# Ring swaps on VectorE, idle-time products on TensorE, table loads behind gates, and the merged tail tiles moved, in an FFT-and-MLP kernel

## The chip, the core and the metric

The program runs on one core of one Trainium2 chip. The core has TensorE (PE in the profile, its weight loads PEld), VectorE (DVE), ScalarE (ACT), GpSimd (POOL) and the queue engine SyncE (SP), and 16 DMA engines that serve transfers issued from SP and from POOL. The metric is the device time of one execution in microseconds (us). Before the change the median of 13 runs is 872.5 us (871.04 to 877.49).

## What is computed

Inputs are x (8 batches of 3008 x 256), complex 256 x 256 weights with biases, and the two matrices of a hidden layer of 2048. Per batch: a real FFT over the 3008 positions, a complex linear layer, a soft threshold, an inverse FFT; then a two-layer network with a squared ReLU on all 24064 rows.

```
X  = rfft(x, axis=1)
Yr = Xr @ w_r - Xi @ w_i + b_r
Yi = Xr @ w_i + Xi @ w_r + b_i
Y  = sign(.) * max(|.| - 0.01, 0)          # on Yr and Yi
y  = irfft(Y).reshape(24064, 256)
out = (s * relu(y @ w_in)**2 + b) @ w_out
```

## The kernel before

The FFT of 3008 = 94 x 32 positions is done as matrix products. A table `A_t` (first DFT over 94), block tables `F_t` and `F_2` (forward over 32, with twiddles), `T_t` (inverse over 32) and `C_t` (inverse over 94) are constants in DRAM. `F_c` and `T_c` are their compact forms as loaded; `place_f` copies `F_c` into `F_t` on ScalarE and into `F_2` on VectorE, `place_t` copies `T_c` into `T_t` on VectorE.

**The first batch** goes through `first_batch`, with nothing beside it. x comes in four chunks (`emit_load_x`, GpSimd's queue); for each chunk 16 products (L320) make `ut`, which ScalarE and VectorE move out of PSUM (L158, L162). SyncE loads everything else at the same time: the weights `w_st`, the biases, `F_c`, `T_c`, the identity and so on, with no wait between them. After the last chunk stand `place_f`, `place_t`, and then 12 steps, each with `mix` (L357), `fwd_dft` (L388), a soft threshold (`m` on ScalarE, L393, and `z` on VectorE, L395), `inv_dft` (L406), and later turns and last DFTs (L421, L438). In `mix` the result `g` leaves PSUM on VectorE (L367) in two steps of three, and on ScalarE (L364) in the third. GpSimd makes `W_g`, `low` and `high` from the weights and biases in between, and loads x of the second batch and `w_in`, `w_out` behind a one-element copy that waits for `T_c`.

**The steady part** is a list of 48 row tiles of the network. A tile has 16 slots; in a slot stand two products of the first layer (L689), the ReLU (L696 on ScalarE), its square (L703 on VectorE or L700 on ScalarE, whichever a running count `load` finds less busy), and four products of the second layer for the tile before (L758). The FFT of later batches is cut into small units that `schedule` spreads over these slots: `s1_units` (first DFT), `s23_units` (forward DFT, complex mix, threshold, inverse DFT, in 12 rounds), `s4_units` (last DFT). In `s23_units`, `mix_unit(i)` ends with four VectorE operations on a buffer `ring` (L563, L568, L569, L570), whose result `t` is brought into another layout `z` by four DMAs of 32 KB each on SyncE's queue (L576): rows 64j.. of half r go to rows 64r.. of half j. `inv_unit(i)` multiplies `z` (L585); its result goes to DRAM (`vd`) and comes back as `vs`. The last rounds of a batch, 10 and 11, have no other unit between them and their `inv_unit` but a few of the same kind.

**The order of tiles** comes from `_tile_order`: three wide tiles per half of the first two batches, then five tiles of 512 rows per batch; what remains of two batches together makes two tail tiles of 512 and 384 rows, which follow in the next free place. The last two tails stand at the very end. A tail tile stores its result in many small DMAs (L742), a main tile in two of 128 KB per pair of sub-tiles (L722). Each engine runs its instructions in program order; SyncE issues its DMAs in order too.

Of the kernel before, what the change touches and what calls it, by code (L numbers as in the profile page):

```python
# [9 lines left out]
F16 = mybir.dt.float16  # L10
# [4 lines left out]
P = 128  # L15
# [57 lines left out]
def _tile_order(nb):  # L73

    tiles = []
    rest = []
    for b in range(nb):
        if b < 2:  # L80
            for h in range(2):
                tiles += [("wide", b, (h, lo), w) for lo, w in ((0, 32), (32, 32), (64, 30))]
            continue
        tiles += [("main", b, j, 512) for j in range(5)]
        pr, half = divmod(b, 2)
        if half == 1:
# [8 lines left out]
def kernel(  # L95
# [82 lines left out]
    def emit_load_x(b):  # L178
        xv = x[b].rearrange("(n1 n2) d -> n1 (n2 d)", n2=N2)
        for c in range(N2 // XCH):  # L180
# [3 lines left out]
            )  # L184
            x16[(b, c)] = t


    A_t = cpool.tile([P, 96], F16, name="A_t")
    nc.sync.dma_start(out=A_t[0:N1, :], in_=A_d)
# [14 lines left out]
    nc.sync.dma_start(out=F_c.rearrange("p q r k -> p q (r k)"), in_=F_d)  # L204
    b_h = cpool.tile([P, D], F16, name="b_h")
    nc.vector.memset(b_h, 0.0)

# [4 lines left out]
    nc.sync.dma_start(out=T_c, in_=T_d)  # L212

    nc.sync.dma_start(out=sel_t, in_=S_d)
    eye_t = cpool.tile([P, P], F16, name="eye_t")
    nc.sync.dma_start(out=eye_t, in_=E_d)
    C_t = cpool.tile([96, 96], F16, name="C_t")
    nc.sync.dma_start(out=C_t, in_=C_d)

    b_st = rpool.tile([P, 2, D], F32, name="b_st", tag="rt")  # L220
    for i, bv in enumerate((b_r, b_i)):
        nc.sync.dma_start(out=b_st[:, i], in_=bv.unsqueeze(0).to_broadcast([P, D]))
# [5 lines left out]
    nc.sync.dma_start(out=s_bc, in_=moe_s.unsqueeze(0).to_broadcast([P, 1]))  # L228
    nc.sync.dma_start(out=bb_bc, in_=moe_b.unsqueeze(0).to_broadcast([P, 1]))
# [12 lines left out]

    neg_lam = cpool.tile([P, 1], F32, name="neg_lam")
    nc.vector.memset(neg_lam, -LAM)
    ones = cpool.tile([P, P], F16, name="ones")
    nc.vector.memset(ones, 1.0)
# [21 lines left out]
    def blocks(t):  # L268
        return t.rearrange("p q (r a k) -> p q r a k", r=2, a=2)
# [5 lines left out]
    def place_f():  # L275
        for a in range(2):
            r = slice(64 * a, 64 * a + 64)
            nc.scalar.copy(out=blocks(F_t)[r, :, :, a], in_=F_c[r])

            for h, f in enumerate(F_2):  # L280
                q = slice(h * H, h * H + H)
                nc.vector.tensor_scalar_mul(
                    out=blocks(f)[r, :, 0, a], in0=F_c[r, q, 1], scalar1=-1.0
                )
                nc.vector.tensor_copy(out=blocks(f)[r, :, 1, a], in_=F_c[r, q, 0])

    def place_t():
        for i in range(4):
            r = slice(32 * i, 32 * i + 32)
            c = 64 * (i % 2)  # L290
            nc.vector.tensor_copy(out=T_t[r, :, c : c + 64], in_=T_c[r])  # L291

    def make_bias():
        ps = other_bank()
# [17 lines left out]
    def first_batch():  # L312
        ut = ypool.tile([P, DC, 96, N2], F16, name="ut", tag="yt")
        last_dve = last_act = None
        for c in range(N2 // XCH):
            for dc in range(DC):
                ps = two_banks()
                for j in range(XCH):
                    lo = j * D + dc * P
                    nc.tensor.matmul(  # L320
                        ps[:, j // 4, (j % 4) * 96 : (j % 4) * 96 + 96],
                        x16[(0, c)][0:N1, lo : lo + P], A_t[0:N1, :],
                        start=True, stop=True,
                    )
# [187 lines left out]
    def s23_units(b):  # L512
# [40 lines left out]
        def mix_unit(i):  # L553
            ps = one_bank().rearrange("p (r e) -> p r e", r=2)
            xt = xf.pop(i)
            for r in range(2):
                for dc in range(DC):
                    nc.tensor.matmul(  # L558
                        ps[:, r, :], xt[:, 2 - r, dc], W_g[:, dc, r],
                        start=(dc == 0), stop=(dc == DC - 1),  # L560
                    )
            t, m = ring[0][:, i % 4], ring[0][:, 4 + i % 2]
            nc.vector.tensor_tensor(  # L563
                out=t, in0=ps, in1=hold[i // 2][:, i % 2].unsqueeze(1).to_broadcast([P, 2, D]),
                op=ALU.add,
            )
# [3 lines left out]
            nc.vector.tensor_tensor(out=t, in0=t, in1=m, op=ALU.subtract)  # L570
            load["dve"] += 1.75

            z = ring[0][:, 6 + i % 6]
            for j in range(2):
                for r in range(2):
                    nc.sync.dma_start(  # L576
                        out=z[64 * r : 64 * r + 64, j], in_=t[64 * j : 64 * j + 64, r]
                    )
            zt[i] = z

        def inv_unit(i):
# [266 lines left out]
```

## Time and profile before

| | value |
|---|---|
| median of 13 runs | 872.5 us |
| the profiled execution: its own time | 871.9 us |
| the profiled execution: its span | 870.0 us |
| PEld / ACT busy | 599.0 / 641.4 us |
| VectorE busy | 694.1 us, 971 instructions |
| SyncE ring DMAs (L576) | 336 |
| HBM traffic | 52.54 MB read, 46.66 MB written |

Busy time is a union per engine; times in a timeline count from the start of the span. In a row of a timeline the first number is the start, the second how long the merged piece lasted, and a bracket at the end tells how long the engine stood idle before it and what ended that. A row of windows gives busy time per engine (with the number of instructions), then the mean granted TensorE clock (1.00 is full), the mean share of the 16 DMA engines and their rate in GB/s. The record of the clock begins 20.6 us into the span; before that the rows read 1.00 whatever it was, and the pace of the products tells.

### The profile page before, as it was taken

To read this page: it belongs to the slowest core of one execution; us is meant where nothing else is said; L and a number is where in the kernel's file an instruction comes from. 1 tells how busy PE (TensorE), PEld (TensorE's weight loads), DVE (VectorE), ACT (ScalarE), POOL (GpSimd) and SP (SyncE) were. 2 spreads that over 40 slices of the span, in tenths; PEclk is the share of its full clock that TensorE was granted. 3 is DMA by queue.
4 is the path that set the end of the run, shared out by engine and by line. 5 is a ranking of instruction groups with operands and counts; after the bars stand their busy time and mean duration, and the time that the engine had idled before them with its cause. 6 is when DMAs were issued, how large, how long until landed. Compare 5 with 4: busy or idle time off the path is not lost.

```text
span 870.0 us, 16955 instructions
## 1 busy us (share of the span) xinstructions
PE 837.9 (96%) x6580; PEld 599.0 (69%) x6580; DVE 694.1 (80%) x971; ACT 641.4 (74%) x848; POOL 32.7 (4%) x53
## 2 busy tenths in 40 slices
PE   4889989999999999999999999999999999999996
PEld 3756766777667766777667776777667777766665
DVE  6788977888778887888878988798877888776664
ACT  4687877687677886787777787787877777666662
POOL 5110000000000000000000000000000000000000
PEclk9999999999999999999999999999999999999999
DMA  8754366423664248522764236623374133411111
GB/s 189 128 121 119 90 157 159 140 57 78 168 151 129 80 113 217 136 64 74 176 169 117 70 97 158 180 86 86 83 193 118 50 86 105 114 31 38 37 39 53
DMA packets 109347, 96.90 MB, mean 111 GB/s; under 512 B 10319, under 2 KB 101715, under 8 KB 107923
## 3 DMA queue, kind: packets, MB, share of 16 engines
q1 hardware_dynamic: 103266, 81.41, 32.7%
q0 software_dynamic: 6000, 14.42, 10.2%
q8 instruction: 51, 0.84, 0.4%
q14 instruction: 30, 0.24, 0.1%
HBM read 52.54 MB, written 46.66 MB: 114 GB/s over the span
## 4 chain that ended last, share of the span: by engine, by line
PE 89%; DMA 4%; ACT 3%; DVE 2%; issue 1%; SPq 0%; POOL 0%; DVEq 0%; POOLq 0%
PE psh L689 36%; PE psa L758 36%; PE psf L558 4%; PE psf L493 3%; DMA ring<-ring 3%; PE psf L529 2%; PE psf L544 2%; PE psf L585 2%; PE psf L638 2%; DMA x<-in_x_dram 1%; ACT rt L696 1%; DVE T_t L291 1%; ACT yt L158 0%; PE psh L357 0%; ACT m L393 0%
## 5 line engine op out<-in xcount | busy, mean ns | idle before, releaser
L696 ACT ACTIVATE rt<-psh 128x1024 f32<-128x1024 f32 (+2 forms) x384 | 387.3, 1009 | 120.7 <-PE psh L689 119.0
L703 DVE TENSOR_TENSOR gt<-rt 128x1024 f16<-128x1024 f32 (+2 forms) x322 | 386.2, 1201 | 110.6 <-ACT rt L696 110.1
L758 PE MATMUL psa<-w_out_t,gt 128*128 128x256 f16 (+1 forms) x3024 | 455.2, 273 | 0.1
L758 PEld LDWEIGHTS <-gt 128*128 128x128 f16 (+1 forms) x3024 | 301.6, 101 | 188.0 <-issue 3.3
L689 PE MATMUL psh<-yt,w_in 128*128 128x512 f16 (+1 forms) x1344 | 398.3, 379 | 0.0
L689 PEld LDWEIGHTS <-w_in 128*128 128x128 f16 x1536 | 143.2, 98 | 26.1 <-issue 1.4
L768 DVE SCALAR_TENSOR_TENSOR ost<-psa,s_bc,bias_bc 128x512 f32<-128x512 f32 (+1 forms) x96 | 70.9, 739 | 8.8 <-PE psa L758 5.7
L158 ACT CAST v<-psf 128x512 f16<-128x512 f32 x79 | 46.1, 583 | 29.0 <-PE psf L585 28.4
L700 ACT ACTIVATE gt<-rt 128x1024 f16<-128x1024 f32 (+2 forms) x62 | 65.5, 1056 | 0.9
L563 DVE TENSOR_TENSOR ring<-psf,s 128x512 f16<-128x512 f32 x84 | 57.6, 686 | 3.3 <-PE psf L558 3.2
L158 ACT CAST u<-psf 96x512 f16<-96x512 f32 x79 | 45.8, 581 | 15.7 <-PE psf L493 15.5
L158 ACT CAST xf<-psf 128x512 f16<-128x512 f32 x78 | 45.7, 586 | 10.4 <-PE psf L529 10.3
L689 PE MATMUL psh<-tail,w_in 128*128 128x512 f16 (+1 forms) x192 | 52.1, 353 | 0.0
L558 PE MATMUL psf<-W_g,xf 128*128 128x256 f16 x336 | 50.4, 273 | 0.0
L158 ACT CAST yt<-psf 128x480 f16<-128x480 f32 (+2 forms) x71 | 36.4, 526 | 10.8 <-PE psf L638 10.7
L493 PE MATMUL psf<-x,A_t 94*96 94x512 f16 x104 | 40.2, 386 | 1.1 <-ACT yt L158 0.5
L585 PE MATMUL psf<-ring,T_t 128*128 128x256 f16 x168 | 33.3, 275 | 6.8 <-DMA ring<-ring 6.5
L569 DVE TENSOR_TENSOR ring<-ring,high 128x512 f16<-128x512 f16 x84 | 35.6, 423 | 2.1
L570 DVE TENSOR_TENSOR ring<-ring 128x512 f16<-128x512 f16 x84 | 35.6, 423 | 2.0
L568 DVE TENSOR_TENSOR ring<-ring,low 128x512 f16<-128x512 f16 x84 | 35.5, 422 | 1.5
L558 PEld LDWEIGHTS <-xf 128*128 128x128 f16 x336 | 32.9, 98 | 3.7
L182 POOL DMA_DIRECT2D x<-in_x_dram x32 | 16.8, 528 | 491.6 <-PE psf L493 455.0
(77 smaller groups left out, 478.3 us busy)
## 6 DMA issues: line engine op xcount, KB each, us to landing
out_dram<-ost SPq DMA_DIRECT2D x152, 128.0 KB
x<-in_x_dram POOLq DMA_DIRECT2D x32, 376.0 KB, 6.5
ud<-u SPq DMA_DIRECT2D x28, 384.0 KB
us<-ud SPq DMA_DIRECT2D x28, 384.0 KB
ring<-ring SPq DMA_DIRECT2D x336, 32.0 KB
vd<-v SPq DMA_DIRECT2D x42, 256.0 KB
vs<-vd SPq DMA_DIRECT2D x14, 768.0 KB
out_dram<-ost SPq DMA_DIRECT2D x16, 120.0 KB
```

The source lines that it names most:

```text
L158: return None, nc.scalar.copy(out=dst, in_=src)
L493: nc.tensor.matmul(ps[0:96, :], A_t[0:N1, :], x16[(b, c)][0:N1, j * D : (j + 2) * D], start=True, stop=True,)
L558: nc.tensor.matmul(ps[:, r, :], xt[:, 2 - r, dc], W_g[:, dc, r], start=(dc == 0), stop=(dc == DC - 1),)
L563: nc.vector.tensor_tensor(out=t, in0=ps, in1=hold[i // 2][:, i % 2].unsqueeze(1).to_broadcast([P, 2, D]), op=ALU.add,)
L569: nc.vector.tensor_tensor(out=m, in0=m, in1=high, op=ALU.min)
L585: nc.tensor.matmul(ps[:, j, :], T_t[:, 2 * i + j, :], z[:, j, :], start=True, stop=True)
L689: nc.tensor.matmul(o, w_in_t[dc][:, mc * P : (mc + 1) * P], r, start=(dc == 0), stop=(dc == DC - 1),)
L696: nc.scalar.activation(out=rt[:, :, 0:w], in_=ps[:, :, 0:w], func=AF.Relu)
L700: nc.scalar.activation(out=gt[:, :, 0:w], in_=rt[:, :, 0:w], func=AF.Square)
L703: nc.vector.tensor_tensor(out=gt[:, :, 0:w], in0=rt[:, :, 0:w], in1=rt[:, :, 0:w], op=ALU.mult)
L758: nc.tensor.matmul(ps[0:size, h, :], gts[(ti, mc // 2)][:, mc % 2, sub * size : (sub + 1) * size], w_out_t[:, mc, :], start=(mc == 0), sto ...
L768: nc.vector.scalar_tensor_tensor(out=ost[0:size, 0:k], in0=ps[0:size, 0:k], scalar=s_bc[0:size], in1=bias_bc[0:size, 0:k], op0=ALU.mult, o ...
```

## The change

Six edits, in the order of the program.

1. `_tile_order`: the two last tail tiles stand ahead of the last three main tiles, so that the program ends with a main tile.
2. `keep_awake(n)`: n products of a tile of ones (128 x 128) into an unused PSUM bank; 44 ahead of the first chunk's products, 18 after each of the first three chunks, 12 after the fourth. The memset of `ones` moves to the front of VectorE's list.
3. The loads of `F_c` and `T_c` get gates: a one-element memset on the destination, which VectorE does after its evictions of the second (`F_c`) and third chunk (`T_c`). What stands behind them on SyncE (identity, `C_t`, broadcast biases, scalars) follows behind `T_c`.
4. `place_f` keeps `F_t` on ScalarE; `F_2` and `T_t` are placed in halves: `place_f_2(0)` at once, `place_t(0)` behind the first `g`, `place_f_2(1)` and `place_t(1)` two steps later.
5. `make_w_g` and `make_bounds` on GpSimd wait for a one-element copy out of `vt` in step 9.
6. In `mix_unit`, rounds 10 and 11 of each batch (i >= H - 2) copy `t` to `z` with four VectorE copies instead of four DMAs, and add 0.13 each to `load["dve"]`. With 7 batches, 56 DMAs become 56 copies.

```diff
-        if rest:
+        if b == nb - 1:
+            tiles[-3:-3] = rest
+        elif rest:
             tiles.append(rest.pop(0))
-    return tiles + rest
+    return tiles
...
+    def keep_awake(n):
+        ps = other_bank()
+        for _ in range(n):
+            nc.tensor.matmul(ps[:, 0:P], ones, ones, start=True, stop=True)
...
+    def emit_load_forward():
+        nc.sync.dma_start(out=F_c.rearrange("p q r k -> p q (r k)"), in_=F_d)
+        nc.sync.dma_start(out=sel_t, in_=S_d)
+    def emit_load_inverse():
+        t_load = nc.sync.dma_start(out=T_c, in_=T_d)
+        with tc.issue_after(t_load.ins):
+            nc.sync.dma_start(out=eye_t, in_=E_d)
...
+    def place_t(h):
+        q = slice(h * H, h * H + H)
...
-            nc.vector.tensor_copy(out=T_t[r, :, c : c + 64], in_=T_c[r])
+            nc.vector.tensor_copy(out=T_t[r, q, c : c + 64], in_=T_c[r, q])
...
+        keep_awake(44)
         for c in range(N2 // XCH):
...
+            with tc.issue_after(last_pe.ins):
+                keep_awake(18 if c < 3 else 12)
+            if c == 1:
+                with tc.issue_after(last_dve.ins):
+                    nc.vector.memset(F_c[0:1, 0, 0, 0:1], 0.0)
+                emit_load_forward()
+            if c == 2:
+                with tc.issue_after(last_dve.ins):
+                    nc.vector.memset(T_c[0:1, 0, 0:1], 0.0)
+                emit_load_inverse()
...
             place_f()
-            place_t()
+            place_f_2(0)
...
-            if i == 6:
-                make_w_g()
-                make_bounds()
+            if i == 0:
+                with tc.issue_after(g_last[0].ins):
+                    place_t(0)
+            if i == 2:
+                with tc.issue_after(g_last[0].ins):
+                    place_f_2(1)
+                    place_t(1)
+            if i == 9:
+                gate = nc.gpsimd.tensor_copy(out=low[0:1, 0, 0:1], in_=vt[0:1, 1, 0, 0:1])
+                with tc.issue_after(gate.ins):
+                    make_w_g()
+                    make_bounds()
...
-                    nc.sync.dma_start(
-                        out=z[64 * r : 64 * r + 64, j], in_=t[64 * j : 64 * j + 64, r]
-                    )
+                    o, a = z[64 * r : 64 * r + 64, j], t[64 * j : 64 * j + 64, r]
+                    if i < H - 2:
+                        nc.sync.dma_start(out=o, in_=a)
+                    else:
+                        nc.vector.tensor_copy(out=o, in_=a)
+                        load["dve"] += 0.13
```

The order of instructions on VectorE after the last chunk of x, before the change (L282 and L285 place `F_2`, L291 places `T_t`, L367 makes `g`, L395 makes `z`; the number behind a name is its buffer):

```order
L282 TENSOR_SCALAR F_165<-F_c 64x12x32
L285 COPY F_165<-F_c 64x12x32
L282 TENSOR_SCALAR F_166<-F_c 64x12x32
L285 COPY F_166<-F_c 64x12x32
L291 COPY T_t<-T_c 32x24x64 x4
L367 TENSOR_TENSOR g_300<-psh,b_g 128x1024
L367 TENSOR_TENSOR g_335<-psh,b_g 128x1024
L395 SCALAR_TENSOR_TENSOR z<-psf,m 128x512 x2
L367 TENSOR_TENSOR g_366<-psh,b_g 128x1024
```

The first four rows stand there twice, for two halves of the partitions. The same place with the change (L298 and L301 place `F_2`, L308 `T_t`, L395 makes `g`, L423 makes `z`):

```order
L298 TENSOR_SCALAR F_156<-F_c 64x12x32
L301 COPY F_156<-F_c 64x12x32
L395 TENSOR_TENSOR g_409<-psh,b_g 128x1024
L308 COPY T_t<-T_c 32x12x64 x4
L423 SCALAR_TENSOR_TENSOR z<-psf,m 128x512
L395 TENSOR_TENSOR g_448<-psh,b_g 128x1024
L423 SCALAR_TENSOR_TENSOR z<-psf,m 128x512
L298 TENSOR_SCALAR F_157<-F_c 64x12x32
L301 COPY F_157<-F_c 64x12x32
L308 COPY T_t<-T_c 32x12x64 x4
L395 TENSOR_TENSOR g_487<-psh,b_g 128x1024
```

Ahead of the first `g` VectorE now has four short placements instead of eight and four long copies; the two halves of `T_t` and the other half of `F_2` stand between the first `g` and the third.

VectorE at the end of the second batch's `s23_units` (rounds 10 and 11), with the change (L601, L606, L607, L608 are the four operations of a round, L618 the swap copies):

```order
L601 TENSOR_TENSOR ring<-psf,s 128x512
L608 TENSOR_TENSOR ring<-ring 128x512
L606 TENSOR_TENSOR ring<-ring,low 128x512
L618 COPY ring<-ring 64x256 x4
L607 TENSOR_TENSOR ring<-ring,high 128x512
L608 TENSOR_TENSOR ring<-ring 128x512
L618 COPY ring<-ring 64x256 x4
L744 TENSOR_TENSOR gt<-rt 128x1024 x2
```

Before, these rows stand in the same order without the copies. On SyncE's queue at this place, before the change, the eight swap DMAs of the two rounds stand between two stores of `ost` and a write of `vd`:

```order
L715 DMA out_dram<-ost 4x30x256 x2
L576 DMA ring<-ring 64x256 x8
L594 DMA vd<-v 128x4x256
L500 DMA ud<-u 96x2048
```

With the change the `vd` write follows the stores at once:

```order
L756 DMA out_dram<-ost 4x30x256 x2
L635 DMA vd<-v 128x4x256
L538 DMA ud<-u 96x2048
```

At the end of SyncE's queue the last 12 stores are now 128 KB ones of main tiles; before, the last 20 were the small ones of the two tail tiles.

More of the change, by code (lines that the diff above doesn't have):

```diff
@@ L185, in emit_load_x @@
             x16[(b, c)] = t
+    ones = cpool.tile([P, P], F16, name="ones")
+    nc.vector.memset(ones, 1.0)
+    def keep_awake(n):
+        ps = other_bank()
+        for _ in range(n):
+            nc.tensor.matmul(ps[:, 0:P], ones, ones, start=True, stop=True)
     A_t = cpool.tile([P, 96], F16, name="A_t")
@@ L203 @@
     F_c = uspool.tile([P, NPAIR, 2, N2], F16, name="F_c", tag="us")
-    nc.sync.dma_start(out=F_c.rearrange("p q r k -> p q (r k)"), in_=F_d)
     b_h = cpool.tile([P, D], F16, name="b_h")
@@ L211 @@
     T_c = uspool.tile([P, NPAIR, 64], F16, name="T_c", tag="us")
-    nc.sync.dma_start(out=T_c, in_=T_d)
-    nc.sync.dma_start(out=sel_t, in_=S_d)
     eye_t = cpool.tile([P, P], F16, name="eye_t")
-    nc.sync.dma_start(out=eye_t, in_=E_d)
     C_t = cpool.tile([96, 96], F16, name="C_t")
-    nc.sync.dma_start(out=C_t, in_=C_d)
     b_st = rpool.tile([P, 2, D], F32, name="b_st", tag="rt")
-    for i, bv in enumerate((b_r, b_i)):
-        nc.sync.dma_start(out=b_st[:, i], in_=bv.unsqueeze(0).to_broadcast([P, D]))
     low = cpool.tile([P, 2, D], F16, name="low")
@@ L227 @@
     bb_bc = cpool.tile([P, 1], F32, name="bb_bc")
-    nc.sync.dma_start(out=s_bc, in_=moe_s.unsqueeze(0).to_broadcast([P, 1]))
-    nc.sync.dma_start(out=bb_bc, in_=moe_b.unsqueeze(0).to_broadcast([P, 1]))
+    def emit_load_forward():
[5 more added lines that the diff above has]
+            nc.sync.dma_start(out=eye_t, in_=E_d)
+            nc.sync.dma_start(out=C_t, in_=C_d)
+            for i, bv in enumerate((b_r, b_i)):
+                nc.sync.dma_start(out=b_st[:, i], in_=bv.unsqueeze(0).to_broadcast([P, D]))
+            nc.sync.dma_start(out=s_bc, in_=moe_s.unsqueeze(0).to_broadcast([P, 1]))
+            nc.sync.dma_start(out=bb_bc, in_=moe_b.unsqueeze(0).to_broadcast([P, 1]))
     w_in_t = [cpool.tile([P, DFF], F16, name=f"w_in_{dc}") for dc in range(DC)]
@@ L244 @@
     nc.vector.memset(neg_lam, -LAM)
-    ones = cpool.tile([P, P], F16, name="ones")
-    nc.vector.memset(ones, 1.0)
     F_t = cpool.tile([P, NPAIR, P], F16, name="F_t")
@@ L278, in place_f, with place_f_2 @@
             nc.scalar.copy(out=blocks(F_t)[r, :, :, a], in_=F_c[r])
[L280 to L283, printed above, removed]
-                )
-                nc.vector.tensor_copy(out=blocks(f)[r, :, 1, a], in_=F_c[r, q, 0])
-    def place_t():
+    def place_f_2(h):
+        q = slice(h * H, h * H + H)
+        for a in range(2):
+            r = slice(64 * a, 64 * a + 64)
+            nc.vector.tensor_scalar_mul(
+                out=blocks(F_2[h])[r, :, 0, a], in0=F_c[r, q, 1], scalar1=-1.0
+            )
+            nc.vector.tensor_copy(out=blocks(F_2[h])[r, :, 1, a], in_=F_c[r, q, 0])
+    def place_t(h):
+        q = slice(h * H, h * H + H)
         for i in range(4):
@@ L319, in first_batch @@
                     lo = j * D + dc * P
-                    nc.tensor.matmul(
+                    last_pe = nc.tensor.matmul(
                         ps[:, j // 4, (j % 4) * 96 : (j % 4) * 96 + 96],
```

1 line of the change is left out of this document (removed).

## The prediction

> **What bounds the kernel now.** I read the page's busy times first, then the timeline of the first 30 us, the waits of TensorE, the windows round those waits, and the timeline of the last 20 us.
>
> ```profile
> span 870.0 us, 16955 instructions
> PE 837.9 (96%) x6580; PEld 599.0 (69%) x6580; DVE 694.1 (80%) x971; ACT 641.4 (74%) x848; POOL 32.7 (4%) x53
> ```
>
> TensorE is the bound: 32.1 us of the 870.0 are all that it stands idle. So the change can win only what TensorE loses: idle time, and time at half clock, which counts as busy. The losses are in three places. The first is the start.
>
> ```profile
> 0.90 0.48 DVE L199 MEMSET b_g<- 128x512 f32 x1 [0.90 <-PEq L832]
> 6.11 1.46 PE L320 MATMUL psh<-A_t,x 94*128 94x96 f16 x16 [6.11 <-DMA x<-in_x_dram]
> 14.24 1.46 PE L320 MATMUL psh<-A_t,x 94*128 94x96 f16 x16 [1.26 <-DMA x<-in_x_dram]
> 15.61 1.20 DVE L162 CAST ut<-psh 128x384 f16<-128x384 f32 x2 [1.52 <-ACT ut L158]
> 16.11 2.95 ACT L278 COPY F_t<-F_c 64x1536 f16<-64x1536 f16 x2
> 16.86 3.38 PE L357 MATMUL psh<-W_t,ut 128*128 128x256 f16 x15 [0.24 <-DVE ut L162]
> 18.35 5.17 DVE L291 COPY T_t<-T_c 32x1536 f16<-32x1536 f16 x4
> 23.55 1.23 DVE L367 TENSOR_TENSOR g<-psh,b_g 128x1024 f16<-128x1024 f32 x1
> 24.83 0.26 PE L388 MATMUL psf<-g,F_t 128*128 128x128 f16 x1 [3.00 <-DVE g L367]
> 25.88 0.69 ACT L393 ACTIVATE m<-psf,neg_lam 128x512 f32<-128x512 f32 x1 [4.58 <-PE psf L388]
> 27.74 1.36 PE L357 MATMUL psh<-W_t,ut 128*128 128x256 f16 x11
> 28.08 1.28 DVE L395 SCALAR_TENSOR_TENSOR z<-psf,m 128x512 f16<-128x512 f32 x2
> 29.28 1.22 DVE L367 TENSOR_TENSOR g<-psh,b_g 128x1024 f16<-128x1024 f32 x1
> ```
>
> The four chunks of x arrive from 6.11 to 14.24, 2.71 apart. `ut` is complete at 15.61 + 1.20 = 16.81. Then VectorE places tables until 23.52, and the first `g`, which TensorE waits for, comes only behind them. The pace of L357 tells the clock: 15 products in 3.38 us (0.22 each) at 16.86, 11 in 1.36 (0.12, the last one's latency included) at 27.74. So the first products ran at half clock, and the stall brought half clock back:
>
> ```profile
> 21.00:24.00 3.00, 0.49 (x3) 0.29 (x3) 2.94 (x4) 0.29 (x1) 3.00 (x4) 1.00 1.05 208
> 24.00:27.00 3.00, 2.17 (x14) 1.69 (x14) 0.83 (x2) 0.69 (x1) 0.58 (x1) 0.51 1.07 216
> ```
>
> The second place is the end of the FFT rounds of each batch. The waits of TensorE on the ring swaps, then windows (the first ahead of a stall, the others round the four largest), then the pieces round the first stall:
>
> ```profile
> PE psf L585 <- DMA ring<-ring: 6.5, 5, 2.5
> ...
> 112.00:123.90 11.90, 11.85 (x87) 8.97 (x85) 10.17 (x17) 10.30 (x16) 0.52 (x1) 1.00 0.48 121
> 123.90:130.00 6.10, 3.62 (x16) 1.85 (x14) 2.59 (x3) 1.79 (x3) 0.00 (x0) 0.72 0.87 224
> ...
> 232.70:239.20 6.50, 4.40 (x19) 2.28 (x18) 2.19 (x3) 2.23 (x4) 0.00 (x0) 0.74 0.72 212
> ...
> 325.00:328.00 3.00, 1.60 (x12) 0.77 (x10) 0.87 (x2) 1.70 (x3) 0.00 (x0) 1.00 0.86 252
> ...
> 534.40:536.50 2.10, 1.39 (x10) 0.66 (x9) 0.56 (x2) 0.98 (x2) 0.00 (x0) 1.00 0.98 323
> ```
>
> ```profile
> 119.71 5.02 SPq L576 DMA_DIRECT2D ring<-ring  x8
> 119.86 0.42 DVE L570 TENSOR_TENSOR ring<-ring 128x512 f16<-128x512 f16 x1
> 126.72 0.39 PE L585 MATMUL psf<-ring,T_t 128*128 128x256 f16 x1 [2.48 <-DMA ring<-ring]
> ```
>
> VectorE has finished round 11 at 120.28, but SyncE takes 5.02 us to issue the eight DMAs (0.63 each), and the product that needs them starts at 126.72. Idle in the four windows: 2.48 + 2.10 + 1.40 + 0.71 = 6.7 us. Half clock behind the two long stalls: (1 - 0.72) x 6.10 + (1 - 0.74) x 6.50 = 3.4 us. Together **10.1 us**.
>
> The third place is the end.
>
> ```profile
> 838.97 0.75 DVE L768 SCALAR_TENSOR_TENSOR ost<-psa,s_bc,bias_bc 128x512 f32<-128x512 f32 x1
> 839.74 1.25 SPq L722 DMA_DIRECT2D out_dram<-ost  x2
> 844.71 1.23 DVE L703 TENSOR_TENSOR gt<-rt 128x1024 f16<-128x1024 f32 x1 [0.24 <-ACT rt L696]
> 845.45 1.02 ACT L696 ACTIVATE rt<-psh 128x1024 f32<-128x1024 f32 x1 [0.77 <-PE psh L689]
> 852.70 14.30 SPq L742 DMA_DIRECT2D out_dram<-ost  x20
> 857.38 6.09 PE L758 MATMUL psa<-w_out_t,gt 128*128 128x256 f16 x52
> 857.58 0.81 ACT L696 ACTIVATE rt<-psh 128x768 f32<-128x768 f32 x1 [0.65 <-PE psh L689]
> 858.69 0.95 DVE L703 TENSOR_TENSOR gt<-rt 128x768 f16<-128x768 f32 x1
> ```
>
> The last product ends at 863.47, SyncE issues small stores until 867.00, and the span ends 3.0 us later: 6.5 us behind TensorE.
>
> **The change, part by part.** I work against the profiled execution, 871.9 us: its span of 870.0 and 1.9 around it. It lies 0.6 under the median of 872.5.
>
> Ring swaps. Eight DMAs per batch become eight VectorE copies of 64 x 256, which the trace has not; the nearest row is a strided copy of 64 x 384:
>
> ```profile
> L285 DVE COPY F<-F_c 64x384 f16<-64x384 f16 x4 | 1.0, 246 | 0.0
> ```
>
> It has half as many elements again, so I expect 0.25 us at most, and nothing excludes half of that; I take 0.25, so 1.0 per round and 2.0 per batch. Round 11 then has its `z` at 120.28 + 2.0 = 122.3, and TensorE asked for it from 126.72 - 2.48 = 124.2. VectorE's idle time in 112 to 123.9 is 1.73, and behind it lie 3.5 in the next 6.1, so the copies fit; if that cover were gone they would cost 7 x 2.0 = 14 us of VectorE's time, not TensorE's, as squares wait in a pool of 15. The `load` entries move an eviction or two per batch to ScalarE, whose share is 74%: nothing. SyncE loses 56 issues, so `vd` goes out sooner: nothing, as TensorE has no wait on `vs` in the profile. Gain 10.1; bounds 5 (half of the waits come back on the copies) and 11.
>
> x and the gates. While x arrives the DMA engines share their time; later x and the weights have them alone (queue, packets, MB, share: first 3 to 13.1 us, then 17.5 to 26):
>
> ```profile
> q0 software_dynamic: 443, 1.53, 76.1%
> q1 hardware_dynamic: 718, 1.04, 30.1%
> ```
>
> ```profile
> q0 software_dynamic: 496, 1.73, 105.0%
> ```
>
> x is q0. Of the 1.04 MB on q1 about half (`F_c`, `T_c` and what follows) is now gated: 0.5 x 30.1% x 10.1 = 1.5 us, so the last chunk comes at 12.7. The chunk's products at full clock take half of their 1.46, of which half lies ahead of the first eviction: 0.35. `ut` is ready at 12.7 + (16.81 - 14.24) - 0.35 = 14.9, 1.9 earlier. Gated, `F_c` is asked for after the second chunk's evictions, about 10.7, and I expect it near 14 to 15, just in time; every us later is a us of VectorE and ScalarE. `T_c` comes 2 us behind it, and GpSimd's second x with it, about 1 us later than now; but it is read only after the twelve steps: nothing.
>
> Idle-time products. `ones` is now VectorE's first memset, and `b_g`, which was, was done at 0.90 + 0.48 = 1.4 with more to write. 44 products of 128 columns take 44 x 0.106 = 4.7 us at half pace (half of 3.38/16 each), so until 6.1 at the latest, when the first chunk lands: hidden. 18 at full pace take 1.0, beside 0.7 for a chunk: 1.7 in a spacing of about 2.2, hidden. The last 12 (0.7) lie under the evictions.
>
> Tables in halves. From 14.9 VectorE has four placements for `F_2` (under 4 x 0.25; they overlap, 0.8), then `g`, whose product is ready at 15.9: done at 17.2. ScalarE's `F_t`, started 0.7 ahead of `ut` as now, takes 2.95, until 17.2. So the first L388 could start at 17.2 instead of 24.83, 7.6 earlier. But then VectorE pays: half of `T_t` (2.6), `z` 0.6 (half of the 1.28), `g` 1.2, `z` 0.6, half of `F_2` 0.8, half of `T_t` without GpSimd's work beside it (4 x 0.47 = 1.9, by the row below), then the `g` that now starts at 29.28: 17.2 + 7.7 = 24.9. That is **4.4** earlier; the bounds are 0.6 (below) and 7.6. What is late next is VectorE in the twelve steps. GpSimd's `W_g` of step 9 is first read in the second batch's rounds, which the plan starts at slot 22 of the tiles: nothing.
>
> How fast `T_t` is placed beside GpSimd is the soft number:
>
> ```profile
> 18.64 1.20 POOL L238 DMA_DIRECT2D w_out_t<-in_moe_w_out_dram x1
> ...
> L291 DVE COPY T_t<-T_c x4: 865/1198/1865, 18.4 to 22.7; 32x1536 f16<-32x1536 f16 x4
> ```
>
> The first copy took 1.87 and lay beside GpSimd issuing loads, the fastest 0.87. With the change `place_t(0)` again lies beside such issues: halves at 0.43 to 0.93, so 1.7 to 3.7; I take 2.6. The Trainium skill, "SBUF — State Buffer", "SBUF: two separate sides", says that VectorE's two-port modes and GpSimd share one pair of ports under an exclusive lock, where the later one is fully blocked. By that the upper end would hold, and the sum would be 1.1 us higher; the trace agrees in the 1.87.
>
> The end. The last product is then followed by one eviction (0.75), two issues (1.25) and the 3.0 us of landing and close: 5.0 instead of 6.5. Against it the last square chain is longer, 1.02 + 1.23 instead of 0.81 + 0.95 (0.5), on which the last products wait. Gain **1.0**, bounds 0 and 1.5.
>
> Sum: 871.9 - 10.1 - 4.4 - 1.0 = **856.4 us**.
>
> **The rivals.**
> - VectorE's backlog eats the start. `T_t` costs 3.7, `F_c` is a us or two late: the start gains 1.5, 859.3 us. For it: VectorE's placements and its first `g` stand without a gap from 18.35 to 24.78, and all of that work is still there. Chance 0.17.
> - The start gains all 7.6, as ScalarE, idle 4.58 us ahead of its first threshold at 25.88, runs ahead and VectorE's idle pieces take the placements: 853.2. Chance 0.13.
> - The clock does not hold. Then a chunk costs 1.46 + 18 x 0.106 = 3.4 us of TensorE, more than the arrivals, and the last chunk's products start at 6.11 + 3 x 3.4 = 16.3 instead of 12.7. The start keeps about 0.6: 860.2. For it: TensorE was busy 1.46 of 2.71 and stayed cold. Against it: 1.7 of 2.2 is more. The Trainium skill, "TensorE: Matmul & The Clock Gate", speaks on both sides: "Part 1: The HAM clock gate" gives full clock after about 3.4 us of sustained work, which agrees with the 3.38 us ahead of the full-clock row at 21; "A second HAM failure mode" has many short idle times between groups bring half clock again. Chance 0.07.
> - The swap is not what is waited for, or the copies come late behind squares: half of the ring's 10.1 stays, 861.5. Against it: `t` was ready 6.4 us ahead of the product. Chance 0.08.
> - Slower: a copy that moves data across partitions costs like `T_t`'s, 0.87 and more. Eight then need 7 us where VectorE has 1.7 to spare, TensorE waits on squares some 5 us in each of 7 batches: 35 us lost, 10 not won, 871.9 - 5.4 + 25 = 891. It decides from about 0.5 us a copy (1.7 + 15.5/7 = 3.9 over eight). Chance 0.03.
> - The change hardly acts (gates and copies give back what they win): 871. Chance 0.02.
>
> **How the numbers follow.** The forecast has 0.50 and the time 856.4. The range goes from the better start with the ring's 11, less a little, to the half-won ring with some more lost at the start: 850.5 to 862.5. Left out are two rivals at once and the last two. Within 0.2% (1.7 us, about what a measurement of this kernel can tell from no change): 0.02; slower 0.03; faster 0.95.
>
> **What would show it.** No wait of L585 on ring swaps in rounds 10 and 11, and full clock near 126 and 236; L618 copies at 0.25 or less. The last chunk's products at 12.7 and 0.05 apart; the first L388 near 17, the third `g` near 25. The last product 5 us ahead of the end. Wrong would be: L585 or L689 waiting for VectorE in the rounds; copies over 0.5; `F_2` waiting for `F_c` beyond 15; products of x at 0.09 apart.

## The result and the profile after

The changed kernel takes **854.21 us** (median of 11 runs, 854.11 to 855.72) where the kernel before took 873.53 (median of 48 runs, 870.39 to 879.04): a ratio of 0.978, 95% interval 0.977 to 0.9796. Forecast were 856.4 us in a range of 850.5 to 862.5. The profiled execution has a span of 852.4 us against 870.0, 17.6 less.

Two lines of the page: the span, then the busy times.

```profile
span 852.4 us, 17140 instructions
...
PE 836.9 (98%) x6690; PEld 602.6 (71%) x6690; DVE 698.0 (82%) x1025; ACT 643.3 (75%) x856; POOL 32.5 (4%) x54
```

TensorE is idle for 15.5 us instead of 32.1, and is as busy as before although 110 products of ones came in. What it still waits for, in us in total, times, and the longest:

```profile
PE psf L416 <- ACT F_t L291: 1.4, 1, 1.4
PE psh L385 <- ACT g L392: 1.1, 1, 1.1
PE psa L196 <- DVE ones L190: 1.0, 1, 1.0
PE psh L338 <- DMA x<-in_x_dram: 1.0, 2, 0.6
```

The ring, 6.5 us before, is gone from this list, and so is the wait of 3.0 for the first `g`. Four lines that the change renumbered are needed here: L338 are the products of x, L416 `fwd_dft`, L395 `g` on VectorE, L626 the products of `inv_unit` on `z`. The start, rows of the timeline on four engines:

```profile
1.04 4.88 PE L196 MATMUL psa<-ones 128*128 128x128 f16 x44 [1.04 <-DVE ones L190]
6.35 0.99 PE L338 MATMUL psh<-A_t,x 94*128 94x96 f16 x16 [0.43 <-DMA x<-in_x_dram]
12.52 0.85 PE L338 MATMUL psh<-A_t,x 94*128 94x96 f16 x16
14.90 2.96 ACT L291 COPY F_t<-F_c 64x1536 f16<-64x1536 f16 x2 [0.95 <-DMA F_c<-dft_fwd]
15.82 1.23 DVE L395 TENSOR_TENSOR g<-psh,b_g 128x1024 f16<-128x1024 f32 x1
16.96 1.44 DVE L308 COPY T_t<-T_c 32x768 f16<-32x768 f16 x4
17.35 2.19 POOL L184 DMA_DIRECT2D x<-in_x_dram  x4 [0.34 <-issue]
17.91 0.23 PE L416 MATMUL psf<-g,F_t 128*128 128x128 f16 x1 [1.42 <-ACT F_t L291]
22.84 1.45 DVE L308 COPY T_t<-T_c 32x768 f16<-32x768 f16 x4
24.32 1.23 DVE L395 TENSOR_TENSOR g<-psh,b_g 128x1024 f16<-128x1024 f32 x1
```

The first L416 comes 6.9 us earlier (17.91 for 24.83), the third `g` 5.0 earlier (24.32 for 29.28), and the first ReLU of the network 5.6 earlier (53.38 for 58.98). That last figure cuts the span in two, and the text below uses it for every kernel: what lies ahead of the first ReLU is the start; what lies behind it was 811.0 us and is 799.0, and holds the ring and the end.

The windows round the places of the first two long stalls (TensorE, weight loads, VectorE, ScalarE, GpSimd, clock, DMA share, GB/s), then the group of the new copies:

```profile
118.00:124.00 6.00, 6.00 (x43) 4.10 (x42) 4.96 (x6) 4.71 (x7) 0.00 (x0) 1.00 0.81 217
...
218.00:224.00 6.00, 6.00 (x46) 4.45 (x45) 5.24 (x9) 5.61 (x9) 0.52 (x1) 1.00 0.85 192
```

```profile
L618 DVE COPY ring<-ring 64x256 f16<-64x256 f16 x56 | 12.4, 222 | 0.9
```

TensorE is busy throughout and at full clock where it stood for 2.48 and 2.10 us and then ran at half. A copy takes 0.222 us. Last the end:

```profile
839.12 7.85 PE L799 MATMUL psa<-w_out_t,gt 128*128 128x256 f16 x68
847.01 0.75 DVE L809 SCALAR_TENSOR_TENSOR ost<-psa,s_bc,bias_bc 128x512 f32<-128x512 f32 x1 [2.31 <-PE psa L799]
```

The last product ends at 839.12 + 7.85 = 846.97, 5.4 us ahead of the end of the span; it was 6.5.

### The profile page after: what moved, and what is told of

Read it like the earlier page. It is cut to its first block, busy times and chain, and to the rows that moved or that the text cites. A ratio compares the mean times of both kernels' runs of the same rounds, so it can differ in the third digit from the quotient of the medians.

```text
span 852.4 us, 17140 instructions
## 1 busy us (share of the span) xinstructions
PE 836.9 (98%) x6690; PEld 602.6 (71%) x6690; DVE 698.0 (82%) x1025; ACT 643.3 (75%) x856; POOL 32.5 (4%) x54
## 4 chain that ended last, share of the span: by engine, by line
PE 90%; DVE 4%; ACT 3%; DMA 2%; issue 1%; POOL 0%; DVEq 0%; ACTq 0%; POOLq 0%
PE psa L799 37%; PE psh L730 37%; PE psf L596 4%; PE psf L531 3%; PE psf L567 2%; PE psf L582 2%; PE psf L626 2%; PE psf L679 2%; DVE gt L744 1%; DMA x<-in_x_dram 1%; ACT rt L737 1%; DVE g L395 1%; ACT yt L160 1%; DMA F_c<-dft_fwd 0%; ACT vs L160 0%
## 5 line engine op out<-in xcount | busy, mean ns | idle before, releaser
L601 DVE TENSOR_TENSOR ring<-psf,s 128x512 f16<-128x512 f32 x84 | 57.6, 686 | 3.5 <-PE psf L596 3.4
L160 ACT CAST xf<-psf 128x512 f16<-128x512 f32 x82 | 48.0, 586 | 11.1 <-PE psf L567 11.1
L160 ACT CAST yt<-psf 128x480 f16<-128x480 f32 (+2 forms) x76 | 38.5, 519 | 14.3 <-PE psf L679 14.3
L607 DVE TENSOR_TENSOR ring<-ring,high 128x512 f16<-128x512 f16 x84 | 35.6, 424 | 2.2
L608 DVE TENSOR_TENSOR ring<-ring 128x512 f16<-128x512 f16 x84 | 35.5, 423 | 1.9
L606 DVE TENSOR_TENSOR ring<-ring,low 128x512 f16<-128x512 f16 x84 | 35.5, 422 | 1.5
L679 PE MATMUL psf<-C_t,vs 96*128 96x96 f16 x448 | 32.9, 205 | 0.0
```

Source lines behind the costliest of these rows:

```text
L160: return None, nc.scalar.copy(out=dst, in_=src)
L601: nc.vector.tensor_tensor(out=t, in0=ps, in1=hold[i // 2][:, i % 2].unsqueeze(1).to_broadcast([P, 2, D]), op=ALU.add,)
L679: nc.tensor.matmul(ps[:, j * 96 : (j + 1) * 96], vs[(b, h)][:, k, ec * P : (ec + 1) * P], C_t, start=True, stop=True,)
```

## The experiments

Each kernel ran in a series beside the kernel before (medians 872.6 to 873.8). The ratio is to that series. The difference to the changed kernel is of medians from different series, so under a microsecond it is believed only where the trace shows the same.

| kernel | us, median | ratio, 95% interval | span of the profiled run | first ReLU at | behind it |
|---|---|---|---|---|---|
| before | 873.53 | | 870.0 | 58.98 | 811.0 |
| changed | 854.21 | 0.978 (0.977 to 0.9796) | 852.4 | 53.38 | 799.0 |
| e1 ring alone, on the kernel before | 861.36 | 0.9857 (0.9829 to 0.9885) | 860.0 | 59.95 | 800.0 |
| e2 changed, ring by DMA | 865.56 | 0.9905 (0.9874 to 0.9937) | 860.9 | 53.42 | 807.5 |
| e10 changed, four rounds copied | 857.29 | 0.9815 (0.9787 to 0.9843) | 855.7 | 53.32 | 802.4 |
| e3 changed, no products of ones | 855.85 | 0.9796 (0.9766 to 0.9827) | 853.4 | 54.43 | 799.0 |
| e5 changed, no gates on loads | 854.62 | 0.979 (0.9764 to 0.9817) | 852.6 | 53.78 | 798.8 |
| e6 changed, tables up front | 856.85 | 0.9811 (0.9785 to 0.9837) | 854.6 | 55.49 | 799.1 |
| e7 changed, W_g early | 859.74 | 0.9843 (0.9815 to 0.9871) | 857.7 | 58.76 | 798.9 |
| e11 W_g late alone, on the kernel before | 869.75 | 0.9965 (0.9942 to 0.9988) | 866.9 | 57.36 | 809.5 |
| e4 changed, old end | 855.32 | 0.9789 (0.9762 to 0.9816) | 853.3 | 53.27 | 800.0 |
| e8 changed, F_t in halves | 854.66 | 0.9791 (0.9765 to 0.9818) | 853.3 | 54.31 | 799.0 |
| e9 changed, F_c asked for sooner | 854.19 | 0.979 (0.9764 to 0.9816) | 852.4 | 53.51 | 798.9 |
| e12 e8 and e9 together | 854.8 | 0.9794 (0.977 to 0.9818) | 851.7 | 52.62 | 799.1 |

### The ring

**e1**, the ring part alone, on the kernel before:

```diff
-                    nc.sync.dma_start(
-                        out=z[64 * r : 64 * r + 64, j], in_=t[64 * j : 64 * j + 64, r]
-                    )
+                    o, a = z[64 * r : 64 * r + 64, j], t[64 * j : 64 * j + 64, r]
+                    if i < H - 2:
+                        nc.sync.dma_start(out=o, in_=a)
+                    else:
+                        nc.vector.tensor_copy(out=o, in_=a)
+                        load["dve"] += 0.13
```

> The kernel before with the ring swaps of rounds 10 and 11 on VectorE, and nothing else changed. Theory (the forecast's first term, now with the copies at the 0.22 us that the trace after shows): 10.1 us faster than before, ratio 0.988, bounds 5 to 11; no wait of the round's last product on a ring DMA, and no 0.7 of granted clock near 126 and 236. Rival 1 (the ring pays all that the start does not): 12 to 14 us faster, ratio 0.985, because smaller waits of the other batches and of the chain behind them go too. Rival 2 (the copies only pass the wait on to VectorE): 5 us faster, with waits of the round's last product or of the first network products on VectorE.

Measured: 11.6 us below its series, ratio 0.9857; behind the first ReLU 11.0 less. Rival 2 falls: no wait on the ring is left. Between the theory (10.1) and rival 1 (12 to 14) the medians do not decide, as the interval of the ratio means 10.0 to 14.9 us. The products that stood in the kernel before start at 124.93 and 229.44 here. Windows round them:

```profile
124.00:130.00 6.00, 6.00 (x44) 4.05 (x42) 5.04 (x6) 4.93 (x8) 0.00 (x0) 1.00 0.93 213
...
229.00:235.00 6.00, 6.00 (x43) 4.05 (x42) 4.52 (x5) 4.28 (x6) 0.00 (x0) 1.00 0.57 178
```

TensorE is busy throughout and at full clock. VectorE, which was busy for 1.90 of 3.10 us and 1.51 of 3.00 round those stalls in the kernel before, works 5.04 and 4.52 of 6.

**e2**, the same lines put back into the changed kernel.

> The changed kernel with all ring swaps as DMAs again, all else as changed. Theory (the parts add up): 10.1 us slower than the changed kernel, so 7.5 us faster than before by the spans (5.6 at the start, 1.1 at the end, some 0.8 that neither has), ratio 0.990 to 0.992; the waits on ring DMAs of 2.5 and 2.1 us are back near 110 and 220. Rival (the parts hide one another: with a quicker start the swaps meet other transfers, and are waited for less): 5 us slower than the changed kernel, ratio 0.985.

Measured: 865.56, which is 11.4 above the changed kernel and 7.4 below its series: with e1's 11.6 that makes 19.0 of the 19.3. The parts add up as far as the medians tell, each to some 2.5 us either way; the rival's 5 us is out. But in the profiled run of e2 the stall has another sequel than in the kernel before. The product behind the swap, then the windows round it:

```profile
121.23 0.28 PE L623 MATMUL psf<-ring,T_t 128*128 128x256 f16 x1 [2.46 <-DMA ring<-ring]
```

```profile
118.50:121.50 3.00, 0.54 (x4) 0.29 (x4) 1.90 (x2) 0.76 (x1) 0.00 (x0) 1.00 0.86 200
121.50:124.50 3.00, 3.00 (x23) 2.07 (x21) 0.78 (x2) 2.10 (x3) 0.00 (x0) 1.00 0.95 259
```

The stall is as long as before (2.46 for 2.48), and this time no half clock follows it. The six runs of e2 have spans of 860.9 to 865.8 with mean clocks of 0.998 to 0.994, the longer the lower. Only one of them has a trace, but the spread says that the same stalls are followed by half clock in one run and not in another. The 3.4 us of half clock in the forecast's sum was one draw.

**e10**, the copies in four rounds of twelve, not two (`if i < H - 4:`), to see how much room VectorE has left.

> The changed kernel with the swaps of rounds 8 to 11 on VectorE, not only 10 and 11: 8 more copies of 0.22 per batch, 1.8 us more of VectorE's time and 8 fewer DMAs on SyncE. Theory A (VectorE's slack hides the copies, and rounds 8 and 9 were never waited for): within 0.6 us of the changed kernel. Theory B (the slower rival's mechanism: VectorE's slack in the rounds is used up, and each further microsecond is TensorE's): 7 x 1.8 = 12.6 us slower at most, 4 us or more.

Measured: 857.29, so 3.1 us slower (3.3 by the spans). Between the two theories: a quarter of the 12.6 us of added copies comes through. The waits that are new:

```profile
PE psf L531 <- DVE ring L601: 1.3, 1, 1.3
PE psf L626 <- DVE ring L601: 0.8, 1, 0.8
```

These two single waits are 2.1 of the 3.3 us. TensorE waits there until VectorE has moved a result out of PSUM (L601), not on squares as in the slower rival. So something near that rival's mechanism sets in at single places: VectorE's slack there ends near where the change stops.

### The start

**e3**, without `keep_awake`.

> The changed kernel without the products of ones. Theory A (the clock is worth what it takes from the chain of x to the first g, and little more): the last chunk's 16 products take 1.46 instead of 0.85, of which half lies ahead of the first eviction, and the 8 products ahead of the first g take 1.7 instead of 0.9; F_t, which the first L416 waited for until 17.86, is not touched: 0.5 to 1.5 us slower than the changed kernel, and full clock comes only near 20. Theory B (half clock stays on through the twelve steps, whose products then bind): 3 us or more slower. Theory C (nothing in the start waits for TensorE): within 0.3 us.

Measured: 855.85, 1.6 slower; first ReLU 1.05 later. Theory A, at its upper end. Rows of PE, then of VectorE:

```profile
12.90 1.44 PE L337 MATMUL psh<-A_t,x 94*128 94x96 f16 x16 [0.52 <-DVE ut L164]
14.97 3.93 PE L382 MATMUL psh<-W_t,ut 128*128 128x256 f16 x16 [0.62 <-DVE ut L164]
...
17.22 1.23 DVE L392 TENSOR_TENSOR g<-psh,b_g 128x1024 f16<-128x1024 f32 x1 [1.00 <-PE psh L382]
```

The 16 products of a chunk take 1.44 for 0.85, the first products of `mix` run at half pace, and VectorE waits 1.00 for them before the first `g`.

**e5**, the gates taken off: `F_c`, `T_c` and what follows are issued ahead of the first chunk's products.

> The changed kernel with F_c, T_c and what follows them loaded at once, as before, without the two gates. Theory A (the gated megabyte held x back, as the forecast has it): the last chunk's products start 1.5 to 1.7 later than 12.52, near 14.1; F_t no longer waits 0.95 for F_c, so the first L416 comes only 0.7 to 1.0 later than 17.91, and the kernel is 0.7 to 1.6 us slower than the changed one. Theory B (x is quicker for other reasons than the gates): the last chunk near 12.5, the first L416 up to 0.9 earlier, up to 0.9 us faster.

Measured: 854.62, and the first ReLU 0.4 later: between the two theories. The rows:

```profile
13.34 0.85 PE L340 MATMUL psh<-A_t,x 94*128 94x96 f16 x16 [0.64 <-DMA x<-in_x_dram]
15.31 2.95 ACT L291 COPY F_t<-F_c 64x1536 f16<-64x1536 f16 x2 [0.56 <-DMA F_c<-dft_fwd]
```

The last chunk starts 0.82 later, half of what theory A had. And `F_c`, issued at 3.92 instead of 11.04, lands at 15.3, later than with its gate. The gates are worth 0.4 us.

**e6**, `place_f_2(1)`, `place_t(0)` and `place_t(1)` moved up behind `place_f_2(0)`.

> The changed kernel with all of F_2 and T_t placed ahead of the first g, as before; GpSimd's W_g still late. Theory A (VectorE's work sets the start, as the forecast has it: what is placed later is paid later): the first L416 comes 2.5 to 3.5 later than 17.91, but the third g, which had the same work ahead of it, within 1 us of 24.32; 0 to 1 us slower than the changed kernel. Theory B (the order itself is worth most of the start's gain): third g 2.5 us later or more, 2.5 to 3.5 us slower. In both the T_t copies stay at 0.35 us, if they were slow before because of GpSimd's arithmetic, and go to 0.43 to 0.93 if the issue of loads beside them was it.

Measured: 856.85, 2.6 slower; first ReLU 2.1 later. The rows:

```profile
16.75 3.08 DVE L308 COPY T_t<-T_c 32x768 f16<-32x768 f16 x8
...
25.79 1.21 DVE L398 TENSOR_TENSOR g<-psh,b_g 128x1024 f16<-128x1024 f32 x1
```

The first L416 starts at 21.14, 3.2 later, as both theories had it; the third `g` 1.5 later. It lies between A and B: the placements are paid for in either order, but ahead of the first `g` they leave TensorE idle (2.00 and 1.70 us in two pieces) so that half clock comes once more (a product each 0.11 behind 21.2, for 0.055). The copies stay at 0.35 to 0.45 us beside GpSimd issuing x from 17.02 to 19.27.

**e7**, W_g and the bounds made right behind the weights' loads again:

```diff
-            if i == 9:
-                gate = nc.gpsimd.tensor_copy(out=low[0:1, 0, 0:1], in_=vt[0:1, 1, 0, 0:1])
-                with tc.issue_after(gate.ins):
+            if i == 6:
+                with tc.issue_after(w_last.ins):
                     make_w_g()
                     make_bounds()
```

> The changed kernel with GpSimd's W_g and bounds right behind the weights' loads again, as before (from about 21.9), beside the second half of T_t at 22.84. Theory A (VectorE's copies of T_t are slowed by GpSimd's arithmetic): that half takes 1.7 to 3.7 us instead of 1.45, the third g comes 0.3 to 2.3 later than 24.32, and the kernel is 0.3 to 2 us slower than the changed one. Theory B (the copies were slow in the kernel before for another reason: their size, ScalarE beside them, or the issue of loads): 1.45 stays, within 0.3 us.

Measured: **859.74, 5.5 us slower**; first ReLU 5.4 later. Theory A has the cause, and its size was far too small. Rows of VectorE and GpSimd, then windows:

```profile
21.63 1.30 POOL L277 TENSOR_TENSOR W_g<-w_st 128x512 f16<-128x512 f32 x1
22.86 1.28 POOL L278 TENSOR_TENSOR W_g<-w_st 128x512 f16<-128x512 f32 x1
...
21.85 2.42 DVE L298 TENSOR_SCALAR F<-F_c 64x384 f16<-64x384 f16 x1
24.19 0.75 DVE L301 COPY F<-F_c 64x384 f16<-64x384 f16 x1
...
28.23 1.22 DVE L395 TENSOR_TENSOR g<-psh,b_g 128x1024 f16<-128x1024 f32 x1
```

```profile
25.00:29.00 4.00, 0.00 (x0) 0.00 (x0) 3.92 (x7) 0.00 (x0) 1.89 (x2) 0.68 1.06 212
29.00:32.00 3.00, 2.49 (x18) 2.12 (x18) 1.75 (x3) 1.22 (x2) 0.00 (x0) 0.50 1.07 213
```

A placement of 0.25 us that begins 0.2 behind GpSimd's first operation lasts 2.42, until the second one is over. The third `g` is late by 3.9, TensorE does nothing from 25 to 29, and half clock follows. This kernel is a harsher test than the old place of W_g: of the two operations at 21.63 and 22.86, the kernel before had one at 9.27, while x arrived.

**e11**, the same gate on W_g put into the kernel before, and nothing else.

> The kernel before with GpSimd's W_g and bounds held back to the end of the twelve steps, and nothing else changed (tables still up front, swaps by DMA, old end). Theory A (GpSimd's arithmetic blocks VectorE's copies between SBUF tiles, whatever else is there): the four T_t copies take 4 x 0.72 = 2.9 us instead of 5.17, the first L388 comes 2.3 earlier than 24.83, and the kernel is 2 to 2.5 us faster than before, ratio 0.997. Theory B (the forecast's: W_g later is worth nothing by itself): within 0.5 us. Theory C (it is worth the 5.5 us that it is worth in the changed kernel): 4 us or more faster, ratio 0.995.

Measured: 869.75, ratio 0.9965: 2.9 us below its series, with an interval of 1.0 to 5.1 that holds theories A and C. The trace speaks for A: the first L388 starts at 22.84, 2.0 earlier than before, and the first ReLU comes 1.6 earlier. Another 1.5 lies behind the first ReLU, where this kernel changes nothing. (GpSimd's order also changed behind the gate: `w_in` and `w_out` went out ahead of three of the four chunks of the second x.) Rows:

```profile
17.20 0.95 DVE L285 COPY F<-F_c 64x384 f16<-64x384 f16 x1
...
21.57 1.22 DVE L367 TENSOR_TENSOR g<-psh,b_g 128x1024 f16<-128x1024 f32 x1
```

The four copies of `T_t` take 2.25 (from 19.29), not 5.17. One copy of `F_2` takes 0.95 for 0.24; GpSimd was issuing `w_out` from 16.88 to 18.08.

### The end

**e4**, the tail tiles last again.

> The changed kernel with the tail tiles at the end again, as before. Theory (the forecast's third term): 1.0 us slower than the changed kernel, last product to end of span 6.5 instead of 5.4, SyncE's 20 small stores the last issues. Rival (the end is set by how long the last store takes to land, whichever it is): no difference beyond 0.3 us. A second way: 1.5 us or more, since the network's first of the tail tiles also had a wait of its own.

Measured: 855.32, 1.1 slower; 1.0 more behind the first ReLU. The theory. The last product's row:

```profile
840.71 6.09 PE L797 MATMUL psa<-w_out_t,gt 128*128 128x256 f16 x52
```

It ends at 846.80, 6.5 ahead of the end of the span; SyncE issues small stores until 850.33.

### Versions that might be better

The first L416 of the changed kernel waits for `F_t`, and `F_t` for `F_c`. **e8** places the second half of `F_t` behind the second threshold:

```diff
-            nc.scalar.copy(out=blocks(F_t)[r, :, :, a], in_=F_c[r])
+            nc.scalar.copy(out=blocks(F_t)[r, q, :, a], in_=F_c[r, q])
...
             if i == 2:
+                with tc.issue_after(m_last[0].ins):
+                    place_f(1)
```

> The changed kernel with F_t placed in halves too: ScalarE places pairs 0 to 11 ahead of the first L416 and pairs 12 to 23 behind the second threshold. Theory A (ScalarE's chain F_t, g, m ahead of the first z is what the start waits for): the first L416 comes near 17.1 instead of 17.91, the first z 1.0 to 1.5 earlier than 19.64, the third g 1.0 to 1.5 earlier than 24.32, and the kernel 0.8 to 1.5 us faster than the changed one, near 853. Theory B (the second half of F_t pushes the third threshold, which now waits for ScalarE): within 0.3 us.

Measured: 854.66, no gain. The steps themselves follow theory A: first L416 at 17.11, first `z` at 18.47, 1.2 earlier. Then, on VectorE, PE and in the windows:

```profile
20.98 0.95 DVE L302 COPY F<-F_c 64x384 f16<-64x384 f16 x1
23.86 1.22 DVE L397 TENSOR_TENSOR g<-psh,b_g 128x1024 f16<-128x1024 f32 x1
...
25.13 0.27 PE L418 MATMUL psf<-g,F_t 128*128 128x128 f16 x1 [2.91 <-DVE g L397]
```

```profile
25.00:27.00 2.00, 1.87 (x15) 1.68 (x15) 0.77 (x3) 0.69 (x1) 0.00 (x0) 0.50 1.02 205
```

A placement now falls beside the issue of `w_out` (20.65 to 21.85) and takes 0.95, so the third `g` is only 0.5 earlier; TensorE, done sooner, waits 2.91 for it in one piece, and half clock takes back more than was won.

**e9** gates `F_c` behind the first chunk (`if c == 0:`).

> The changed kernel with F_c's load gated behind the first chunk's evictions instead of the second's. Theory A (F_t starts when F_c has landed): F_c lands about 2 us sooner, ScalarE starts F_t behind its last eviction, near 14.3 instead of 14.90, and the kernel is 0.3 to 0.6 us faster. Theory B (the transfers share one rate: F_c sooner makes the last chunk later): the last chunk's products start 0.4 to 1 later than 12.52, and the kernel is within 0.3 us or up to 0.5 slower.

Measured: 854.19, nothing. Issued at 8.20 instead of 11.04, `F_c` lands no sooner:

```profile
15.04 2.95 ACT L291 COPY F_t<-F_c 64x1536 f16<-64x1536 f16 x2 [0.85 <-DMA F_c<-dft_fwd]
```

**e12** has both.

> Both at once: F_t in halves, and F_c's load behind the first chunk's evictions. Theory A of both: 1.2 to 2 us faster than the changed kernel, near 852.5. Otherwise as the better of the two alone.

Measured: 854.8. Its profiled run is the shortest of all, 851.7, because the clock held there:

```profile
24.69 0.22 PE L418 MATMUL psf<-g,F_t 128*128 128x128 f16 x1 [2.29 <-DVE g L397]
```

```profile
24.50:26.50 2.00, 1.81 (x22) 1.57 (x22) 1.18 (x3) 1.16 (x2) 0.00 (x0) 1.00 1.05 211
```

Of the six runs of e12 the profiled one took 853.47 and another 854.21, both at a mean clock of 0.999; the other four took 854.76 to 855.5, at 0.996 to 0.997. No version beats the change.

## Why the prediction held, and where it did not

The forecast was 2.2 us above the median. By the stages of the profiled execution:

| term | forecast | by the stage | by the experiments |
|---|---|---|---|
| ring swaps | 10.1 (5 to 11) | 11.0 | 11.6 (e1), 11.4 (e2) |
| start | 4.4 (0.6 to 7.6) | 5.6 | |
| end | 1.0 (0 to 1.5) | 1.0 | 1.1 (e4) |
| sum | 15.5 | 17.6 | 19.3 (medians) |

The profiled execution of before lay 1.6 under the median of all 48 runs; that is the rest between 17.6 and 19.3. So the change was worth 3.8 us more than forecast, and the low base took 1.6 of it back: that the time came as near as 2.2 us is in part luck.

**Ring swaps: right, a little small.** The wait was for the swap DMAs, and the copies took their place without one; how much of it was SyncE's issuing and how much the landing, no run separates. The 0.222 us of a copy lies under the 0.25 taken. The sum had four windows; the 0.9 beyond it was not traced to single waits. How much half clock hangs on the stalls differs from run to run (e2).

**Products of ones: right.** They end at 1.04 + 4.88 = 5.92, ahead of the first chunk, and are worth 1.05 us by the first ReLU, 1.6 by the medians (e3). The forecast gave them no term of their own but the 0.35 of a chunk's products; the half pace of the first products of `mix`, on which the first `g` waits 1.00 without them, was left out.

**Gates: over-rated.** The forecast moved the last chunk 1.5 earlier by them; taking them off costs 0.8 there and 0.4 in the time (e5). The last chunk of x landed 11.3 us after its issue before, 9.6 with the change, 9.8 without the products of ones (e3) and 10.4 without the gates. So x comes 0.9 earlier even without the gates, and why stays open. The landing of `F_c` "near 14 to 15, just in time" was 14.90, and ScalarE had waited 0.95 for it.

**Tables in halves: right in sign and course.** First L416 at 17.91 against "could start at 17.2", third `g` at 24.32 against 24.9, and VectorE does pay in the steps. The mis-sized terms are the placements: `T_t` took 1.44 and 1.45, forecast 2.6 and 1.9, bounds from 1.7. (The 1.9 is 4 x 0.47 "by the row below", but half of that row's 0.87 is 0.43, which gives 1.7.) These 1.6 us outweigh the 0.7 by which `F_t` was late (done at 17.86, not 17.2). Of the 1.2 us that the start won beyond the forecast, 0.6 is there at the third `g`; the other 0.6 comes behind it and was not traced.

**W_g: the step that failed.** The prediction has "GpSimd's `W_g` of step 9 is first read in the second batch's rounds [...]: nothing". That the delay costs nothing is right. But W_g's old place cost the start, and the prediction put the slow `T_t` copies of the kernel before down to GpSimd issuing loads. The four copies of the kernel before one by one, then GpSimd's arithmetic beside them:

```profile
18.35 1.86 DVE T_t L291
20.23 1.52 DVE T_t L291
21.76 0.88 DVE T_t L291
22.65 0.86 DVE T_t L291
...
19.84 1.49 POOL L265 TENSOR_TENSOR W_g<-w_st 128x512 f16<-128x512 f32 x1
21.32 0.90 POOL L257 TENSOR_SCALAR low<-b_st 128x512 f16<-128x512 f32 x1
22.21 1.78 POOL L266 TENSOR_SCALAR W_g<-W_g 128x512 f16<-128x512 f16 x1
```

The issue of `w_out` ended at 19.84, so only the first copy lies beside it, and its end beside W_g; the other three lie beside W_g and `low` alone. In e11, without W_g, each takes 0.55. The prediction counted the absence of W_g for the second half of `T_t` alone (1.9 in place of 2.6). With W_g early the changed kernel loses 5.4 of the 5.6 us of its start (e7); the other edits of the start rest on it, though e7 has one operation more in the way than the kernel before. By itself, with the tables still up front, the late W_g brings 1.6 by the first ReLU and 2.9 by the medians (e11). The edits of the start do not add up: taken away one at a time (e3, e5, e6, e7) they cost 1.05 + 0.40 + 2.11 + 5.38 = 8.9 us by the first ReLU, where 5.6 are to be had.

The rule of the Trainium skill that the prediction weighed there ("SBUF — State Buffer", "SBUF: two separate sides": VectorE's two-port modes and GpSimd hold a shared pair of ports by an exclusive lock, the later one is blocked) agrees with e7, where an operation of 0.25 us takes 2.42 beside GpSimd's arithmetic. The prediction applied it to the issue of loads, which gave 3.7 for the half that took 1.44 beside x's issue.

**End: right**, 5.4 us behind the last product for 5.0 forecast, and 1.0 won.

**Rivals.** VectorE's backlog did not eat the start, as the backlog itself shrank. The clock held: a chunk's products took 0.85 from the second chunk on. The slower rival did not come at 0.222 us a copy, yet e10 shows TensorE waiting for VectorE 8 copies further. The rival's 891 counts the ring's 10 us as won; with "10 not won", as its text has it, the sum would be 901.

## What to carry over

Before pricing a slow copy, look at what every other engine did during each single one: here it was GpSimd's arithmetic, and 5 us of it, that nobody was waiting for, decided what the rest of the start was worth. Price a stall of a few microseconds on TensorE with the half clock that may follow, and expect this part to differ between runs. When an engine that still has room takes over work from a queue that has none, count how far the room goes: two rounds left no wait that weighs, the next two cost a quarter of their time.

## What the runs showed of the hardware

- GpSimd's arithmetic between SBUF tiles holds up VectorE's copies between SBUF tiles: 0.25 us became 2.42 beside two operations of 1.3 with two inputs each (e7), and 0.67 to 0.87 beside those with one; the four `T_t` copies took 5.17 in the kernel before, 2.25 without it (e11, where `w_out`'s issue had moved away from them too). VectorE's operations out of PSUM were not slowed: `g` took 1.23 in the kernel before beside W_g's last operations, and 1.23 in the changed kernel without them.
- GpSimd issuing a load can hold up such a copy too. Beside the issue of `w_out` one took 0.95 for 0.24 and ended 0.1 behind that issue (e8, e11); beside the four chunks of x a copy lost 0.1 at most (e6). The first `T_t` copy of the kernel before took 1.86 for 0.55, beside the issue of `w_out` and the first 0.4 us of W_g; no run separates the two.
- The same stall of 2.5 us was followed by half clock in the kernel before and not in e2; 2.91 was in e8, 2.29 was not in e12. The Trainium skill, "TensorE: Matmul & The Clock Gate", "Part 1: The HAM clock gate", says that activity is counted in windows that run freely, whatever the kernel does. The spread agrees; its idle window of about 3.4 us is longer than the 2.48 that sufficed here, and in e6 two idle pieces of 2.00 and 1.70 us were enough.
- While x arrives, a transfer that is issued sooner need not land sooner: `F_c` issued at 3.92 (e5), 8.20 (e9) and 11.04 was there at 15.3, 15.0 and 14.9.
